# Pauses between the steps of the filling work, and a shorter second phase, in an FFT and GEGLU kernel

## The chip, the core and the metric

The kernel runs on one core of one Trainium2 chip. A core has a matrix engine (TensorE, PE in the profile, with its weight loads as PEld), three engines for elementwise work (VectorE or DVE, ScalarE or ACT, GpSimd or POOL), and SyncE (SP), from which this kernel issues nearly all its DMAs. Each engine works through a queue of its own, in the order in which the program wrote the instructions; the engines wait for each other by semaphores. The metric is the device time of one execution, in microseconds (us).

## What is computed

Two branches work on one input x of 8192 tokens by 448 channels, and their results are multiplied:

```python
x = A_x
xn = _layernorm(x, axis=-1)
s = _A_ref(xn, A_w1, A_b1, A_w2, A_b2)     # FFT over tokens, block MLP, inverse FFT
g = _silu(_B_ref(xn, B_w_gate, B_w_up, B_w_down))
return x + s * g

def _B_ref(x, w_gate, w_up, w_down):
    return (_gelu(x @ w_gate) * (x @ w_up)) @ w_down
```

`_A_ref` takes the real FFT over the 8192 tokens, runs a complex two-layer MLP in four blocks of 112 channels on every frequency (a ReLU between the layers, soft shrinkage by 0.01 behind them) and transforms back. `_B_ref` is a gated feed-forward network of width 1792. All products are formed from float16 pairs (a high and a low part), so that one float32 product is three matmuls or so.

## The kernel before

**Main work.** `ffn` runs the feed-forward network as 16 chunks of 512 tokens, in two passes over its width: p = 0 with 8 blocks of 128 columns, p = 1 with 6. Most chunks use Strassen-like products (`unit`), whose sums are formed on DVE, ACT and POOL, and a down projection (`down`, `down2`). Its tiles are `xta` and `xtb` (transposed tokens, fetched from the DRAM tensor `xts`), `wt` and `dw` (weights), `u`, `v`, `gl`, `wt` (intermediate sums), `h` (hidden values), `pt` and `th` (outputs). Its PSUM banks are six, named `bk`.

**Filling work.** Everything else is written into the gaps of the main work, with two PSUM banks named `bf`:

- Phase 1: `chunk1(c)` for c = 2 to 17 normalizes a chunk (`stats`, `norm`, tiles `st`, `x`, `xs`), forms its sums and stores them to `xts` (`factors`, tiles `sf`, `sx`), and does the first FFT stage (`stage1`: matmuls `bf<-xs,m`, results `ysb`, stored to `t1`). Chunks 16 and 17 are chunks 0 and 1 again, for `xts` alone. A chunk begins every DT = 40 us of the plan. Beside it `weights` prepares the second pass: `gu_block(b, 1)` for three blocks, `down_weights(1)`, and `prep_mlp` (MLP weights `w1t`, `w2t`); each of these calls begins when the one before it has ended.
- Phase 2 begins when both are done: `zero` for the first frequencies, then 64 calls of `group`, one every dt = (END2 - t0) / 64 (second FFT stage `bf<-sm,y`, MLP, shrinkage, third stage `bf<-vt,sm`).
- Phase 3: 32 calls of `tiles3` (last stage `bf<-u,mt`, product with the other branch in tile `g`, sum with x, store), one every dt = (END3 - t0 - 12) / 32. The last two leave `s4`, with which the main work's closing chain forms the last output.

**Who sets the order.** The whole program is written by one Python object, `Pace`, called the plan below. Every piece of work is a generator (a task). `Pace` keeps a modelled time for each engine, takes the task whose time comes first, lets it issue a few instructions, and puts it back: a bare `yield` means "go on when what I have just issued has ended in the model", `yield t` means "not before t", and `yield event` waits for another task. On the chip nothing of this exists: what remains is the order of the instructions in each engine's queue, and semaphores for true dependences. If the chip is later than the model at some place, an instruction may stand at the head of its queue with its operand not ready, and all behind it stand too. `SLACK` = 1.0 (line 26) is a margin of that kind for the `bf` banks (lines 415, 591 and 1571). `Either` (line 185) gives some elementwise operations to DVE or POOL, whichever would end first in the model. SP's DMAs go through the same plan.

**Lines that the change touches.** `Pace.__init__`, `spawn` and `run` (lines 54 to 101); `stage1` (585); END1, END2, END3 (1734); the loop of `phase3` that spawns `tiles3` (1802); `weights` (1914); `first` (1936), which spawns `chunk1`. Since every instruction is issued by the helper `Engine`, the profile gives line 180 (L180) for all of them; groups are told apart by tile names.

Of the kernel before, what the change touches and what calls it, by code (L numbers as in the profile page):

```python
# [21 lines left out]
NG = 16  # L22
CH = 4

PL = 2
SLACK = 1.0
BLK = ((0, 1), (1, 1)) + tuple((f, 2) for f in range(2, 14, 2))
NBK = len(BLK)

# [19 lines left out]
class Pace:  # L49
# [2 lines left out]


    def __init__(self):
        self.now, self.last, self.n, self.heap = 0.0, 0.0, 0, []
        self.free, self.seen, self.dma = {}, {}, 0.0


# [1 line left out]
        self.n += 1  # L60
        heapq.heappush(self.heap, (t, self.n, task))

    def spawn(self, gen, at=None):
        done = Event()

        def whole():
            yield from gen
            self.set(done)

        self.push(whole(), self.now if at is None else at)  # L70
        return done

    def then(self, fn, at=None):
# [12 lines left out]
    def run(self):  # L86
        while self.heap:
            t, _, task = heapq.heappop(self.heap)
            self.now = max(self.now, t)
            self.last = self.now  # L90
            try:
                y = next(task)
            except StopIteration:
                continue
            if isinstance(y, Event):
                if y.done:
                    self.push(task, self.now)
                else:
                    y.waiting.append(task)
            else:  # L100
                self.push(task, self.last if y is None else max(self.now, y))


    @staticmethod
# [279 lines left out]
def afno_geglu_kernel(ctx, tc, x, gu, wd, mlp, b1, b2, c_m, c_mt, c_small, out):  # L384
    nc = tc.nc
    pace = Pace()
# [27 lines left out]
    BX = BY = BD = Banks(pace, [psp.tile([128, 512], F32, name=f"bk{n}", bufs=1) for n in range(6)])  # L414
    BF = bank("bf", 2, SLACK)

    def part(bank_, *shape):

        n = int(np.prod(shape[1:]))
        v = bank_[0:shape[0], 0:n]  # L420
        return v.rearrange("p (a b) -> p a b", a=shape[1]) if len(shape) == 3 else v
# [25 lines left out]
    def block(f):  # L447
        return [f0 <= f < f0 + n for f0, n in BLK].index(True)

# [135 lines left out]
    def stage1(c, q, xs):  # L585
        if c >= PL:
            yield ev("lo", c, q)
        yield ev("m", c)
        m4 = EV["m4", c]
        ysb = yield from YS.get()  # L590
        yield pace.now + SLACK
        for a in range(2):
            b = yield from BF.get()
            py = part(b, 128, D)
            hi, lo = xs[:, a, 0], xs[:, a, 1]
            T.matmul(py, m4[:, 2 * q + a, 0, :], hi, start=True, stop=False)
            T.matmul(py, m4[:, 2 * q + a, 0, :], lo, start=False, stop=False)
            T.matmul(py, m4[:, 2 * q + a, 1, :], hi, start=False, stop=True)
            yield
            ph = py.rearrange("p (h d) -> p h d", h=2)  # L600
            S.activation(ysb[:, a, :, 0], ph, AF.Copy, scale=2.0 ** -16)
            yield
            V.scalar_tensor_tensor(ysb[:, a, :, 1], ph, 2.0 ** -16, ysb[:, a, :, 0], op0=ALU.mult, op1=ALU.subtract)
            BF.put(b)
        yield
        n2 = CH * c + 2 * q
        for ri in range(2):
            Q.dma_start(t1[:, ri, n2:n2 + 2, :], ysb[64 * ri:64 * ri + 64].rearrange("p a h s d -> p a (h s d)"))
        YS.put(ysb)

    def chunk1(c):

        yield ev("xl", c)
        yield from stats(c, G)
        yield
        tasks = []
        for q in range(2):
            xs = yield from XS.get()
            for a in (2 * q, 2 * q + 1):
                norm(c, a)  # L620
                yield
            xn = EV["x4", c][:, 2 * q:2 * q + 2, :]
            f = pace.spawn(factors(c, q, xs))
            S.copy(xs[:, :, 0, :], xn)
            yield
            B.tensor_sub(xs[:, :, 1, :], xn, xs[:, :, 0, :])
            pace.then(lambda c=c, q=q: done("lo", c, q))
            mine = [f]
            if c < NG:
                mine.append(pace.spawn(stage1(c, q, xs)))  # L630

            def back(mine=mine, xs=xs):
                for e in mine:
                    yield e
                XS.put(xs)

            tasks.append(pace.spawn(back()))
        yield tasks[0]
        yield tasks[1]
        done("xts", c % NG)  # L640
        X4.put(EV["x4", c])
        ST.put(EV["st", c])
        if c < NG:
            M4.put(EV["m4", c])
# [9 lines left out]
    T1, DT = 84.0, 40.0  # L654
# [11 lines left out]
    def gu_block(b, to):  # L666

        f0, n = BLK[b]
        for i in range(n):
# [867 lines left out]
    def layer1(n, w, z, h):  # L1537
# [32 lines left out]
        e = pace.spawn(other(), at)  # L1570
        yield pace.now + SLACK
        product(p0, 2, 1, False, True)
# [158 lines left out]

            pace.spawn(store())

    END1, END2, END3 = T1 + NG * DT + 12.0, 1480.0, 1780.0

    def phase2():
        yield ev("phase1")
# [36 lines left out]
    def tiles3(c):  # L1774
        yield ev("l3", c)
        t = EV["l3t", c]
        u2, mt = t[0:2]
        o2 = t[3] if c < 2 * NG - 2 else None
        for a in range(2):
            b = yield from BF.get()  # L1780
            p = part(b, 128, D)
            three(p, mt[:, a], u2[:, a, 0:D], u2[:, a, D:2 * D])
            yield
            if o2 is None:
                S.activation(state["last"][0][:, 2 * (c % 2) + a, :], p, AF.Copy, scale=cF)
                BF.put(b)
                yield
                done("s4", 2 * (c % 2) + a)
                continue
            V.scalar_tensor_tensor(o2[:, a, :], p, cF, o2[:, a, :], op0=ALU.mult, op1=ALU.mult)  # L1790
            BF.put(b)
            yield
            B.tensor_add(o2[:, a, :], o2[:, a, :], t[2][:, a, :])
            yield
        P3["u2"].put(u2)
        P3["mt"].put(mt)
        if o2 is not None:
            P3["x2"].put(t[2])
            Q.dma_start(ov[:, 2 * c:2 * c + 2, :], o2)
            P3["g2"].put(o2)  # L1800

    def phase3():
        r2.close()
        p3 = ctx.enter_context(tc.tile_pool(name="p3", bufs=1, side="right"))
        state["last"] = [p3.tile([128, CH, D], F32, name=n) for n in ("s4", "x4l")]
        for name, shape, dt, bufs in (("u2", [128, 2, 2 * D], F16, 3), ("mt", [128, 2, 3, 128], F16, 3),
                                      ("x2", [128, 2, D], F32, 3), ("g2", [128, 2, D], F32, 3)):
            P3[name] = ring(p3, shape, dt, name, bufs)
        n3 = 2 * NG
        order = list(range(n3))  # L1810
        t0 = pace.now
        dt = (END3 - t0 - 12.0) / n3
        pace.spawn(load3(order[0]))
        pace.spawn(load3(order[1]))
        Q.dma_start(state["last"][1], xv[:, CH * (NG - 1):, :])
        for k, c in enumerate(order):
            yield t0 + 10.0 + k * dt
            if k + 2 < n3:
                pace.spawn(load3(order[k + 2]))
            pace.spawn(tiles3(c))  # L1820


    p2 = None
# [90 lines left out]
    def weights():  # L1914

        near = range(PF[0][1])
        pace.spawn(gu_loads(near, 0))
        for b in range(PB[0][1]):
            pace.spawn(gu_block(b, 0))
        combs = pace.spawn(gu_combs(near))  # L1920
        yield ev("w", 1)
        yield pace.spawn(down_weights(0))
        yield combs
        yield 150.0
        for b in range(*PB[1]):
            yield pace.now + 10.0
            pace.spawn(gu_loads(range(BLK[b][0], sum(BLK[b])), 0))
            yield pace.spawn(gu_block(b, 1))
        yield pace.now + 10.0
        yield pace.spawn(down_weights(1))  # L1930
        far_rest()
        yield pace.last + 6.0
        yield pace.spawn(prep_mlp())
        done("weights")

    def first():
        G.memset(mhalf, -0.5)
        pace.spawn(begin())
        pace.spawn(weights())
        yield 0.0  # L1940
        S.activation(fb[:, 4:5], mhalf[:, 0:1], AF.Gelu_apprx_tanh)
        pace.spawn(load_m(0))
        pace.spawn(loads1())
        pace.spawn(ffn())
        tasks = []
        yield 28.0
        done("phase", 1)
        pace.spawn(begin1())
        for c in range(PL, NG + PL):
            done("phase", c - 1)  # L1950
            yield T1 + (c - PL) * DT
            if c > PL + 1:
                yield tasks[-2]
            tasks.append(pace.spawn(chunk1(c)))
        for e in tasks:
            yield e
        yield ev("weights")
        done("phase1")
        yield from phase2()
        yield from phase3()  # L1960
# [21 lines left out]
```

## Time and profile before

| what | us |
|---|---|
| median of three runs | 1845.62 |
| the three runs | 1842.31, 1845.62, 1846.54 |
| profiled execution, its own time | 1843.94 |
| profiled execution, span from first to last instruction | 1842.2 |
| mean granted TensorE clock of the profiled execution | 0.996 |

The profile page lists busy times for each engine; the trace behind it can be asked for stretches of time (busy times of each engine, granted clock, DMA), for waits (who stood for whom), for groups of equal instructions, and for single instructions in order of time. Times within the trace count from the span's start. An arrow `out<-in` names the tiles written and read. In lists of single instructions the first two numbers are start and duration, and brackets hold the idle time ahead of one and what ended it; `SPq`, in the place of an engine, is SyncE's sequencer issuing a DMA. In rows of groups, the numbers behind the bar are busy us in total, mean ns of one, and idle us of the engine just ahead of the group's instructions, with what ended it. Rows of one tile give shortest, median and longest duration in ns, then the first and last start in us.

### The profile page before, as it was taken

The numbers are of one execution on the slowest core, as the hardware profiler recorded it, in microseconds if no ns is written. First come the engines' busy times: TensorE is split into PE (matmuls) and PEld (weight loads), VectorE is DVE, ScalarE is ACT, GpSimd is POOL, SyncE is SP. The second block draws the span as 40 slices with busy tenths as digits, with TensorE's granted clock in tenths as the row PEclk, the third lists the DMA queues.
The fourth block names the chain that finished last, engine by engine and source line by source line (L and its number), as shares of the span: only waits on it lengthen the run. The fifth ranks groups of instructions, "written<-read, shape, count | busy, mean of one in ns | idle before, by whom it ended". The sixth has DMA issues, their size and how long they took to land. (4 is left out here: it accounts for less than half of the span.)

```text
span 1842.2 us, 39141 instructions
## 1 busy us (share of the span) xinstructions
PE 1774.8 (96%) x15649; PEld 1423.5 (77%) x15649; DVE 1423.4 (77%) x2418; ACT 1096.9 (60%) x2105; POOL 582.9 (32%) x629
## 2 busy tenths in 40 slices
PE   6999999999999999999999999999999999999997
PEld 3447567666777777887877899989989898878886
DVE  7867788776866666656767788888888897888888
ACT  4746566655655555566766777677777774434443
POOL 3334444324523313100101233334432342333332
PEclk9999999999999999999999999999999999999999
DMA  7463665586564552132235544543344435999984
GB/s 263 140 168 113 195 193 177 164 233 186 147 165 115 150 155 82 44 92 74 64 114 166 147 104 117 117 104 88 98 103 117 112 97 156 327 297 319 289 311 148
DMA packets 345655, 287.79 MB, mean 156 GB/s; under 512 B 231840, under 2 KB 312736, under 8 KB 345472
## 3 DMA queue, kind: packets, MB, share of 16 engines
q1 hardware_dynamic: 345328, 285.26, 53.9%
q8 instruction: 122, 2.00, 0.4%
q14 instruction: 61, 0.50, 0.1%
q10 hardware_dynamic: 144, 0.03, 0.0%
HBM read 129.47 MB, written 106.61 MB: 128 GB/s over the span
## 5 line engine op out<-in xcount | busy, mean ns | idle before, releaser
L180 PEld LDWEIGHTS <-wt 128*128 128x128 f16 x9350 | 908.7, 98 | 191.6 <-issue 26.6
L180 PE MATMUL bk<-xta,wt 128*128 128x256 f16 (+1 forms) x5190 | 635.2, 276 | 9.2 <-DVE wt L180 4.6
L180 PE MATMUL bk<-xtb,wt 128*128 128x256 f16 x3120 | 382.2, 273 | 7.7 <-ACT v L180 7.7
L180 PE MATMUL bk<-dw,h 128*128 128x448 f16 (+1 forms) x2208 | 375.1, 321 | 9.0 <-DVE h L180 4.1
L180 PEld LDWEIGHTS <-h 128*128 128x128 f16 x2688 | 257.8, 98 | 140.8 <-DVE h L180 5.7
L180 ACT COPY v<-bk 128x512 f32<-128x512 f32 x208 | 121.7, 585 | 100.6 <-PE bk L180 99.3
L180 ACT COPY u<-bk 128x512 f32<-128x512 f32 x208 | 121.2, 585 | 70.9 <-PE bk L180 65.2
L180 POOL TENSOR_TENSOR wt<-wt 128x256 f32<-128x256 f32 x92 | 81.2, 883 | 185.9 <-DVE wt L180 174.4
L180 DVE TENSOR_TENSOR u<-bk,u 128x512 f32<-128x512 f32 x104 | 71.3, 686 | 86.4 <-PE bk L180 85.9
L180 POOL TENSOR_TENSOR zs<-t,zs 112x256 f16<-112x256 f32 (+2 forms) x41 | 35.5, 865 | 303.4 <-ACT zs L180 297.7
L180 ACT ACTIVATE u<-u,fc 128x512 f32<-128x512 f32 (+1 forms) x118 | 77.7, 669 | 62.0 <-DVE u L180 61.6
L180 PE MATMUL bk<-dw,wt 128*128 128x224 f16 (+1 forms) x864 | 103.1, 269 | 8.1 <-DVE pt L180 8.0
L180 POOL TENSOR_TENSOR v<-v,u 128x512 f32<-128x512 f32 x40 | 61.2, 1531 | 156.5 <-ACT v L180 152.5
L180 DVE SCALAR_TENSOR_TENSOR pt<-bk,fb,pt 128x448 f32<-128x448 f32 x112 | 74.7, 677 | 32.9 <-PE bk L180 32.0
L180 ACT CAST h<-wt 128x512 f16<-128x512 f32 (+1 forms) x128 | 68.6, 538 | 48.7 <-DVE wt L180 36.3
L180 ACT ACTIVATE th<-bk,fb 128x448 f32<-128x448 f32 x64 | 40.5, 633 | 85.4 <-PE bk L180 59.8
L180 PE MATMUL bf<-w2t,wn 112*128 112x112 f16 x1512 | 84.9, 213 | 0.0
L180 PEld LDWEIGHTS <-wn 112*128 112x128 f16 x1512 | 80.6, 98 | 2.4
L180 DVE TENSOR_TENSOR v<-bk,v 128x512 f32<-128x512 f32 x104 | 71.0, 683 | 12.9 <-PE bk L180 11.4
L180 POOL TENSOR_TENSOR h<-wt,h 128x512 f16<-128x512 f32 (+1 forms) x50 | 62.8, 1260 | 39.7 <-ACT h L180 37.8
L180 PEld LDWEIGHTS <-w1t 112*112 112x112 f16 x612 | 68.1, 130 | 7.5 <-issue 2.9
L180 DVE TENSOR_SCALAR x<-x,st 128x448 f32<-128x448 f32 x72 | 56.0, 790 | 22.3 <-POOL st L180 22.1
(197 smaller groups left out, 2934.4 us busy)
## 6 DMA issues: line engine op xcount, KB each, us to landing
wst<-in_gu SPq DMA_DIRECT2D x22, 704.0 KB, 5.4
xts<-sx SPq DMA_DIRECT2D x32, 480.0 KB, 2.9
x<-in_x SPq DMA_DIRECT2D x17, 896.0 KB, 5.9
t<-ysb SPq DMA_DIRECT2D x64, 224.0 KB, 3.4
prt<-th SPq DMA_DIRECT2D x64, 224.0 KB, 2.6
pt<-prt SPq DMA_DIRECT2D x64, 224.0 KB, 4.4
u<-t SPq DMA_DIRECT2D x32, 448.0 KB, 5.6
y<-t SPq DMA_DIRECT2D x30, 448.0 KB, 3.5
```

The lines of the kernel that those rows point to most:

```text
L180: return self.pace.issue(self.name, kind, out, ins, lambda: fn(out, *args, **kw))
```

## The change

Each task gets a number `lag`, handed on to the tasks that it spawns unless another is given. A bare `yield` then means "go on `lag` us after what I have just issued has ended in the model". Tasks of the main work, the first two chunks, the weights of the first pass and phase 2 keep lag 0. `chunk1`, `gu_block(b, 1)`, `down_weights(1)` and `prep_mlp` get LAG = 1.0, with all that they spawn (`factors`, `stage1` and others); `tiles3` gets 0.5. In `stage1` the margin ahead of the bank gets the lag too, and behind each bank stands one more pause of that length. END2 goes from 1480 to 1460, so that the calls of `group` follow each other faster and phase 3 begins earlier, while END3 stays at 1780. No instruction is added or taken away.

```diff
--- before.py
+++ after.py
@@ -24,6 +24,7 @@
 
 PL = 2
 SLACK = 1.0
+LAG = 1.0
 BLK = ((0, 1), (1, 1)) + tuple((f, 2) for f in range(2, 14, 2))
 NBK = len(BLK)
 
@@ -52,7 +53,7 @@
 
 
     def __init__(self):
-        self.now, self.last, self.n, self.heap = 0.0, 0.0, 0, []
+        self.now, self.last, self.n, self.heap, self.lag = 0.0, 0.0, 0, [], 0.0
         self.free, self.seen, self.dma = {}, {}, 0.0
 
 
@@ -60,14 +61,14 @@
         self.n += 1
         heapq.heappush(self.heap, (t, self.n, task))
 
-    def spawn(self, gen, at=None):
+    def spawn(self, gen, at=None, lag=None):
         done = Event()
 
         def whole():
             yield from gen
             self.set(done)
 
-        self.push(whole(), self.now if at is None else at)
+        self.push((whole(), self.lag if lag is None else lag), self.now if at is None else at)
         return done
 
     def then(self, fn, at=None):
@@ -88,8 +89,9 @@
             t, _, task = heapq.heappop(self.heap)
             self.now = max(self.now, t)
             self.last = self.now
+            self.lag = task[1]
             try:
-                y = next(task)
+                y = next(task[0])
             except StopIteration:
                 continue
             if isinstance(y, Event):
@@ -98,7 +100,7 @@
                 else:
                     y.waiting.append(task)
             else:
-                self.push(task, self.last if y is None else max(self.now, y))
+                self.push(task, self.last + self.lag if y is None else max(self.now, y))
 
 
     @staticmethod
@@ -588,9 +590,11 @@
         yield ev("m", c)
         m4 = EV["m4", c]
         ysb = yield from YS.get()
-        yield pace.now + SLACK
+        yield pace.now + SLACK + pace.lag
         for a in range(2):
             b = yield from BF.get()
+            if pace.lag:
+                yield pace.now + pace.lag
             py = part(b, 128, D)
             hi, lo = xs[:, a, 0], xs[:, a, 1]
             T.matmul(py, m4[:, 2 * q + a, 0, :], hi, start=True, stop=False)
@@ -1731,7 +1735,7 @@
 
             pace.spawn(store())
 
-    END1, END2, END3 = T1 + NG * DT + 12.0, 1480.0, 1780.0
+    END1, END2, END3 = T1 + NG * DT + 12.0, 1460.0, 1780.0
 
     def phase2():
         yield ev("phase1")
@@ -1817,7 +1821,7 @@
             yield t0 + 10.0 + k * dt
             if k + 2 < n3:
                 pace.spawn(load3(order[k + 2]))
-            pace.spawn(tiles3(c))
+            pace.spawn(tiles3(c), lag=0.5)
 
 
     p2 = None
@@ -1925,12 +1929,12 @@
         for b in range(*PB[1]):
             yield pace.now + 10.0
             pace.spawn(gu_loads(range(BLK[b][0], sum(BLK[b])), 0))
-            yield pace.spawn(gu_block(b, 1))
+            yield pace.spawn(gu_block(b, 1), lag=LAG)
         yield pace.now + 10.0
-        yield pace.spawn(down_weights(1))
+        yield pace.spawn(down_weights(1), lag=LAG)
         far_rest()
         yield pace.last + 6.0
-        yield pace.spawn(prep_mlp())
+        yield pace.spawn(prep_mlp(), lag=LAG)
         done("weights")
 
     def first():
@@ -1951,7 +1955,7 @@
             yield T1 + (c - PL) * DT
             if c > PL + 1:
                 yield tasks[-2]
-            tasks.append(pace.spawn(chunk1(c)))
+            tasks.append(pace.spawn(chunk1(c), lag=LAG))
         for e in tasks:
             yield e
         yield ev("weights")
```

## The prediction

> **What bounds the kernel now.** The first view is the page's table of busy times, for the engine that is nearest to full.
>
> ```profile
> PE 1774.8 (96%) x15649; PEld 1423.5 (77%) x15649; DVE 1423.4 (77%) x2418; ACT 1096.9 (60%) x2105; POOL 582.9 (32%) x629
> ```
>
> TensorE (PE) is busy for 1774.8 of 1842.2 us, and the change takes no matmul away, so only the 67.4 us in which PE is idle, and stretches in which it runs slowly, can be won. The second view cuts the span at the borders of the three phases of the filling work. Its columns are the stretch, its length, the busy time of PE, its weight loads, DVE, ACT and POOL, then the granted clock and the DMAs.
>
> ```profile
> 150.00:490.00 340.00, 322.95 (x2421) 237.78 (x2420) 264.14 (x456) 198.93 (x360) 145.93 (x182) 0.98 0.60 175
> 490.00:742.00 252.00, 249.60 (x1891) 184.67 (x1891) 169.40 (x283) 134.24 (x241) 72.35 (x92) 1.00 0.51 135
> 742.00:1150.00 408.00, 408.00 (x4051) 343.70 (x4049) 293.24 (x517) 278.00 (x566) 68.20 (x64) 1.00 0.38 103
> 1150.00:1537.00 387.00, 381.57 (x4121) 350.61 (x4119) 332.16 (x555) 279.68 (x573) 149.76 (x138) 1.00 0.41 99
> 1537.00:1823.00 286.00, 272.58 (x2421) 234.65 (x2420) 237.38 (x352) 121.36 (x215) 95.60 (x84) 1.00 0.92 294
> 1823.00:1843.00 20.00, 8.12 (x78) 7.38 (x77) 12.83 (x22) 3.62 (x7) 0.00 (x0) 0.88 0.14 46
> ```
>
> Length less PE's time is PE's idle time: 17.1 us in 150 to 490 (5.0%), 2.4 us in 490 to 742 (1.0%), none in 742 to 1150, 5.4 us in 1150 to 1537 (1.4%), 13.4 us in 1537 to 1823 (4.7%), and about 11 us of closing chain. DVE is busy for 78%, 67%, 72%, 86% and 83% of the first five. So a full DVE alone doesn't stop PE: the fullest stretch costs 1.4%, a less full one 5.0%. The third view says what ended PE's idle time between 150 and 742.
>
> ```profile
> PE bf L180 <- DVE ysb L180: 4.0, 4, 1.9
> PE bk L180 <- ACT u L180: 2.7, 2, 1.7
> PE bk L180 <- POOL h L180: 2.6, 1, 2.6
> PE bk L180 <- ACT v L180: 2.1, 1, 2.1
> PE bf L180 <- DVE fx L180: 1.9, 2, 1.7
> PE bk L180 <- DVE h L180: 1.8, 2, 1.3
> PE bk L180 <- DVE wt L180: 1.5, 1, 1.5
> PE bf L180 <- DVE dmx L180: 1.3, 1, 1.3
> PE bf L180 <- DVE mxr L180: 1.2, 1, 1.2
> PE bf L180 <- DVE xs L180: 0.4, 1, 0.4
> ```
>
> The columns are who waited for whom, the sum in us, how often, and the longest. The `bf` rows are matmuls of the filling work itself, at which PE's queue stood: 4.0 + 1.9 + 1.3 + 1.2 + 0.4 = 8.8 us. The `bk` rows are the main work's matmuls, late because ACT, DVE or POOL came to their operand late: 2.7 + 2.6 + 2.1 + 1.8 + 1.5 = 10.7 us. One place in order of time, PE first and DVE second, shows how both arise.
>
> ```profile
> 184.81 0.61 PE L180 MATMUL bk<-xta,wt 128*128 128x256 f16 x4 [1.48 <-DVE wt L180]
> 187.31 1.30 PE L180 MATMUL bf<-xs,m 128*128 128x448 f16 x3 [1.89 <-DVE ysb L180]
> ```
>
> ```profile
> 184.67 2.04 DVE L180 TENSOR_TENSOR xs<-x,xs 128x896 f16<-128x896 f32 x1
> 186.64 0.61 DVE L180 SCALAR_TENSOR_TENSOR ysb<-bf,ysb 128x448 f16<-128x448 f32 x1
> ```
>
> DVE is back to back here. The `ysb` instruction, the last reader of a `bf` bank, starts only at 186.64, and the filling matmul that wants the bank was written into PE's queue on the plan's belief that it would be free. PE, with main work behind, stands for 1.89 us.
>
> **The change part by part.** No instruction is added or removed, and no wait: a pause in the plan only puts a step at a later place in its engines' queues, DMAs and SP's queue included. Nothing is queued behind a pause.
>
> **1. Pauses in the first phase, matmuls of the filling work.** A step written 1 us later finds its operand ready if the chip runs up to 1 us behind the plan; `stage1` gains 2 us before its first matmul, the plain pause at line 591 and the new one behind the bank. The four `ysb` waits, longest 1.9, should go nearly all. `fx`, `dmx` and `mxr` get 1 us against longest waits of 1.7, 1.3 and 1.2. That alone leaves about 1.3 of 8.8 us; new waits of the kind will arise at other places. Bounds: 0 and -8.8; I take two thirds, **-6.0**.
>
> **2. The same pauses, main matmuls.** With filling steps spread, ACT, DVE and POOL meet fewer filling instructions in a row ahead of a main one. It is a matter of order, and DVE's total stays. Bounds: 0 and -10.7; I take less than half, **-4.0**, as only some of these bursts are the filling work's own.
>
> **3. The clock.** Two stretches of the first phase have a low granted clock (the last figure but two).
>
> ```profile
> 184.00:196.00 12.00, 9.31 (x55) 6.50 (x56) 9.34 (x13) 6.55 (x14) 6.07 (x6) 0.72 0.33 93
> 443.00:451.00 8.00, 6.50 (x26) 3.04 (x27) 4.72 (x8) 3.12 (x6) 2.29 (x4) 0.79 0.56 164
> ```
>
> ```profile
> 444.50 0.36 PE L180 MATMUL bk<-dw,h 128*128 128x448 f16 x1 [2.60 <-POOL h L180]
> ```
>
> They cost 0.28 x 12 + 0.21 x 8 = 5.0 us of PE time, and each follows idle PE: 1.48 and 1.89 us in the first, 2.60 us for POOL's `h` in the second. Fewer stalls should leave fewer of these. Bounds 0 and -5.0; I take half, **-2.5**.
>
> The Trainium skill, "TensorE: Matmul & The Clock Gate", section "What's actually happening", has the clock halve after at least one idle window of about 3.4 us. The trace doesn't agree as it stands: no idle piece before these two stretches is longer than 2.6 us. By that rule such short stalls cost no clock, this term would be 0, and the sum below 2.5 us higher.
>
> **4. Later ends in the first phase.** The pauses add up along a task. The last `chunk1` (c = 17) has about 18 pauses in a row: six through `stats`, two at `norm`, four in the first `factors` while it holds the one SF buffer, six in the second and its stores. For the weights: about 31 in each of three `gu_block` calls, 40 in `down_weights(1)`, 25 in `prep_mlp`, or 158 us in all.
>
> ```profile
> 505.16 0.68 DVE L180 SCALAR_TENSOR_TENSOR w2t<-raw,ms,w2t 112x448 f16<-112x448 f32 x1
> ```
>
> ```profile
> L180 PE MATMUL bf<-sm,y x768: 216/219/222, 742.4 to 1509.6; 128*112 128x128 f16 x189, 128*112 128x130 f16 x3
> ```
>
> ```profile
> 790.30 0.83 PE L180 MATMUL bf<-sm,y 128*112 128x128 f16 x12
> ```
>
> The weights now end at 505 and would end near 663, still before the second phase's first matmul at 742.4; that one moves by the chunk's 18 us to about 760. So weight work moves into 490 to 742, where PE is idle for 1.0% only. At worst that stretch takes on the 5.0% of the one before it: 252 x 4.0% = +10.1 us; at best its 2.4 us go. I take **+2.0**, nearest to its own row, since DVE has room there (67%).
>
> Nobody on PE waits for the later chunks:
>
> ```profile
> 195.22 2.32 SPq L180 DMA_DIRECT2D xts<-xs  x4
> ...
> 254.76 4.00 SPq L180 DMA_TRANSPOSE xta<-xts  x1
> ```
>
> The transposed data of chunk 4 are stored by 198 and fetched at 254.76, when the buffer comes free. The cover is some 57 us against about 18 us of pauses; without it, each us of excess would stand on PE.
>
> **5. The denser second phase.** Its groups begin at 790.30 and the last at 1509.6: 719.3 / 63 = 11.42 us a group. A start 18 us later and END2 20 us earlier make that (719.3 - 38) / 63 = 10.81 us, 5.6% more filling work per us. Between 1150 and 1537 half of DVE's work is the filling work's: ten groups from the first row below to the last sum to 182 us, and the ten of the main work to 184.
>
> ```profile
> L180 DVE SCALAR_TENSOR_TENSOR vt<-vt,o 128x448 f16<-128x448 f16 (+1 forms) x35 | 25.8, 737 | 4.6 <-ACT vt L180 4.5
> ...
> L180 DVE TENSOR_TENSOR zs<-t,zs 112x256 f16<-112x256 f32 x9 | 4.2, 466 | 1.4 <-ACT zs L180 1.4
> ```
>
> So DVE goes from 86% to about 88%. Bounds: -1 (the first half starts later) and the third phase's 4.7% over 387 us, 18.2 - 5.4 = +12.8. I take **+2.5**, half as much again as now, because the stretch's own row is the nearest and DVE stays below full.
>
> **6. The third phase, pause 0.5 us and an earlier start.**
>
> ```profile
> L180 PE MATMUL bf<-u,mt x192: 349/352/362, 1558.4 to 1822.5; 128*128 128x448 f16 x192
> ```
>
> ```profile
> PE bk L180 <- DVE pt L180: 6.8, 17, 1.5
> PE bk L180 <- ACT v L180: 5.6, 4, 2.5
> ```
>
> ```profile
> L180 DVE SCALAR_TENSOR_TENSOR g<-bf,ms,g 128x448 f32<-128x448 f32 x60 | 40.5, 677 | 12.4 <-PE bf L180 11.2 <-DMA g<-gsp 1.2
> L180 DVE TENSOR_TENSOR g<-g,x 128x448 f32<-128x448 f32 x42 | 33.4, 796 | 0.6
> ```
>
> END3 stays, so its tiles have 284 us in place of 264.1, 7% fewer per us, and the DMAs (0.92 busy in that stretch) as much relief. `g` is 73.9 us of DVE's work, 26% of 286 us, so DVE falls by about 2 points. PE waits for main operands (`pt`, `v`) here, not for filling matmuls, so the pause itself does little. Bounds: down to the 1.4% of the stretch before it, 4.0 - 13.4 = -9.4, and +3 if pauses push the last tile into the closing chain (some six of 0.5 us). I take **-3.0**.
>
> The choice between DVE and POOL for one instruction (Either) is made afresh with each new time; that can go either way and is left at nothing, inside the bounds of 2 and 5.
>
> **Sum:** -6.0 - 4.0 - 2.5 + 2.0 + 2.5 - 3.0 = -11.0 us. The profiled execution took 1843.94 us (1842.2 span and 1.7 around it), so 1832.9; the median of the three runs, 1845.62, lies 1.7 above it, so **1834.6**, told as 1835.
>
> **The rivals.** *Stalls only move.* DVE's total and PE's order of main work stay, so a burst avoided here meets another there. For it: POOL's and ACT's waits are scattered, no place repeats. Against it: 8.8 us stand at filling matmuls whose steps get later by more than most of those waits. Time: that of before, 1844 to 1846. That the pauses leave the queues' order nearly as it is, since the plan had room there already, ends at the same time.
>
> *The second phase becomes the place that stalls.* Mechanism: at 88% DVE falls behind the plan between 1150 and 1537, main products wait for `u`, `v`, `pt`, and the stretch takes the third phase's rate, +12.8. With half of points 1 to 3 (-6.2) and nothing from the third phase: 1843.9 + 6.6 + 1.7 = 1852, slower. It decides from the point where the stretch gains about 10 us of idle time. For it: 1.4% at 86% beside 4.7% at 83% shows how fast that can turn. Against it: 72% to 86% of DVE has cost only 5.4 us.
>
> *Nearly all of the first phase comes back.* Points 1 to 3 at 85% of their bounds, -20.8, with the other points as above, +1.5: 1826. For it: most `bk` waits too have filling work ahead of them in the queue. Against: point 2 has no rule that protects a main matmul.
>
> **How the numbers follow.** The forecast has 0.50, the full recovery 0.15, stalls that move 0.18, queues left nearly as they are 0.05, the stalling second phase 0.12. A measurement of this kernel tells 0.2%, 3.7 us, from no change. Faster takes the first two and a little of the moving stalls, less the forecast's weak edge: 0.66; same 0.20; slower 0.14. The range 1822 to 1850 takes in the full recovery and what lies between the forecast and the stalling second phase.
>
> **What would show it.** Right: the waits for `ysb`, `fx`, `dmx`, `mxr` under 3 us together; idle PE in 150 to 490 under 9 us; the weights' last `w2t` near 660 and the first `bf<-sm,y` near 760; the first `bf<-u,mt` near 1540 and its stretch under 11 us idle. Wrong: new waits of main matmuls between 490 and 742, over 10 us of idle PE between 1150 and 1537, or a closing chain that is longer than 11 us.

## The result, and the profile after

| | us |
|---|---|
| changed kernel, median of four runs (1817.71 to 1823.30) | 1819.38 |
| kernel before, median of four runs beside it (1842.31 to 1846.54) | 1844.35 |
| ratio, 95% interval | 0.9867, 0.9854 to 0.9881 |
| profiled execution of the changed kernel, its own time and span | 1818.44, 1816.3 |

The change makes the kernel 1.3% faster, 25 us. The forecast was 1835, and the lower end of its range, 1822, lies 2.6 us above the measured time. The page's table of busy times for the changed kernel:

```profile
PE 1768.8 (97%) x15649; PEld 1422.6 (78%) x15649; DVE 1401.5 (77%) x2410; ACT 1098.1 (60%) x2105; POOL 588.0 (32%) x637
```

PE's count is the same; its idle time is 1816.3 - 1768.8 = 47.5 us in place of 67.4. The stretches, cut at this kernel's own phase borders (columns as in the prediction):

```profile
150.00:490.00 340.00, 333.18 (x2547) 248.13 (x2546) 268.37 (x474) 204.57 (x369) 131.13 (x166) 1.00 0.60 174
490.00:735.00 245.00, 244.70 (x1869) 183.04 (x1868) 166.03 (x298) 138.98 (x252) 84.91 (x101) 1.00 0.56 158
735.00:1150.00 415.00, 413.39 (x4115) 348.81 (x4114) 303.34 (x541) 288.37 (x584) 66.53 (x63) 1.00 0.38 101
1150.00:1515.00 365.00, 362.60 (x3936) 333.71 (x3934) 310.68 (x513) 263.18 (x541) 152.25 (x143) 1.00 0.42 103
1515.00:1801.00 286.00, 278.07 (x2475) 239.64 (x2474) 235.12 (x345) 124.94 (x221) 106.20 (x101) 1.00 0.92 292
```

Idle PE is 6.8, 0.3, 1.6, 2.4 and 7.9 us, where it was 17.1, 2.4, 0, 5.4 and 13.4. The low clock of the first stretch (0.98 before) is gone. What PE waited for between 150 and 742:

```profile
PE bk L182 <- ACT u L182: 4.8, 2, 3.4
PE bk L182 <- DVE wt L182: 0.9, 1, 0.9
PE bk L182 <- ACT wt L182: 0.7, 1, 0.7
PE bk L182 <- DVE h L182: 0.3, 1, 0.3
PE bk L182 <- ACT v L182: 0.3, 1, 0.3
```

Not one `bf` row is left: in this stretch PE stands at no matmul of the filling work any more. Rows of tiles and two instructions give the dates of the phases:

```profile
649.24 0.68 DVE L182 SCALAR_TENSOR_TENSOR w2t<-raw,ms,w2t 112x448 f16<-112x448 f32 x1
```

```profile
L182 PE MATMUL bf<-sm,y x768: 217/219/222, 734.8 to 1487.5; 128*112 128x128 f16 x189, 128*112 128x130 f16 x3
```

```profile
787.05 0.83 PE L182 MATMUL bf<-sm,y 128*112 128x128 f16 x12
```

```profile
L182 PE MATMUL bf<-u,mt x192: 352/352/363, 1535.9 to 1800.6; 128*128 128x448 f16 x192
```

The weights end at 649 (505 before). The second phase begins at 734.8, earlier than the 742.4 of before; its groups follow each other every (1487.5 - 787.05) / 63 = 11.12 us (11.42 before). The third phase's matmuls spread over 264.7 us, just as before (264.1).

Idle time leaves out half-clock stretches, so the experiments are compared by **lost time**: for each matmul the time to the next one's start, less the usual step of its shape in the trace of before (109 ns for 256 columns, 189 ns for 448), summed over a phase. "First" runs from 150 us to the first `bf<-sm,y`, "second" from there to the last `bf<-vt,sm`, "third" from there to the last matmul. "Half clock" is the part of the whole loss that is due to a halved clock. How the usual step is taken shifts a sum by up to 1 us.

| kernel | first | second | third | half clock | median us | ratio to before, 95% |
|---|---|---|---|---|---|---|
| before | 29.4 | 10.1 | 20.8 | 5.1 | 1844.35 | |
| the change | 10.9 | 8.2 | 14.0 | 0 | 1819.38 | 0.9867 (0.9854 to 0.9881) |
| e1 pauses of phase 1 alone | 15.1 | 11.5 | 18.0 | 3.4 | 1827.07 | 0.9889 (0.9870 to 0.9907) |
| e2 END2 alone | 28.4 | 9.9 | 23.4 | 5.1 | 1847.80 | 1.0007 (0.9998 to 1.0017) |
| e3 pause in tiles3 alone | 32.0 | 10.1 | 19.8 | 10.2 | 1842.52 | 0.9987 (0.9974 to 1.0000) |
| e4 pauses of chunk1 alone | 16.0 | 10.1 | 30.2 | 8.5 | 1839.27 | 0.9966 (0.9951 to 0.9981) |
| e5 pauses of the weights alone | 18.0 | 17.5 | 22.9 | 8.5 | 1843.35 | 0.9988 (0.9979 to 0.9998) |
| e6 stage1's two pauses alone | 26.6 | 12.2 | 28.4 | 8.5 | 1853.94 | 1.0048 (1.0032 to 1.0064) |
| e7 chunk1's steps without those two | 15.5 | 11.4 | 19.2 | 3.4 | 1829.99 | 0.9924 (0.9908 to 0.9940) |
| e8 two long pauses per chunk | 26.8 | 14.1 | 19.7 | 8.5 | 1843.59 | 0.9993 (0.9978 to 1.0008) |
| e19 weights apart, no pause | 28.2 | 8.3 | 22.1 | 6.8 | 1847.43 | 1.0010 (0.9999 to 1.0021) |
| e12 LAG 0.5 | 28.2 | 15.5 | 17.1 | 10.2 | 1847.93 | 1.0009 (1.0000 to 1.0018) |
| e18 LAG 1.1 | 20.2 | 12.1 | 13.3 | 6.8 | 1834.24 | 0.9935 (0.9921 to 0.9950) |
| e11 LAG 2.0 | 15.3 | 25.1 | 70.7 | 42.7 | 1902.89 | 1.0309 (1.0291 to 1.0326) |
| e9 the change, no pause in tiles3 | 13.2 | 8.3 | 23.0 | 3.4 | 1831.52 | 0.9920 (0.9905 to 0.9935) |
| e20 the change, 0.4 in tiles3 | 14.2 | 8.1 | 11.4 | 3.4 | 1817.74 | 0.9847 (0.9831 to 0.9864) |
| e21 the change, 0.6 in tiles3 | 13.4 | 8.2 | 16.6 | 1.7 | 1822.54 | 0.9873 (0.9858 to 0.9888) |
| e10 the change, END2 1480 | 13.5 | 11.4 | 18.5 | 1.7 | 1834.14 | 0.9933 (0.9919 to 0.9948) |
| e16 the change, END2 1470 | 13.1 | 14.5 | 16.2 | 1.7 | 1827.84 | 0.9904 (0.9887 to 0.9920) |
| e15 the change, END2 1450 | 14.1 | 23.8 | 19.9 | 6.8 | 1843.11 | 0.9987 (0.9976 to 0.9998) |

Each lost time is of one profiled execution, which can lie some us from its kernel's median: e3's took 1848.18 us, 5.7 above, e15's 4.2 above. Each ratio is to runs of the kernel before on the same chip. Eight of these kernels (the change, e1, e9, e10, e15, e16, e20, e21) have PE's order in the first phase in common, and lose 10.9 to 15.1 us there: that is how far one order scatters, and differences below 4 us within a phase say nothing. The lost time of the change and of before differs by 18.5, 1.9 and 6.8 us in the three phases, 27.2 in all, of which some 1.6 go back in the first 84 us.

### The profile page after: what moved, and what is told of

It reads as the page before. It is cut to its first block, busy times and chain, and to the rows that moved or that the text cites. A ratio compares the mean times of both kernels' runs of the same rounds, so it can differ in the third digit from the quotient of the medians.

```text
span 1816.3 us, 39111 instructions
## 1 busy us (share of the span) xinstructions
PE 1768.8 (97%) x15649; PEld 1422.6 (78%) x15649; DVE 1401.5 (77%) x2410; ACT 1098.1 (60%) x2105; POOL 588.0 (32%) x637
## 5 line engine op out<-in xcount | busy, mean ns | idle before, releaser
L182 PEld LDWEIGHTS <-wt 128*128 128x128 f16 x9350 | 907.0, 98 | 181.8 <-issue 18.5
L182 POOL TENSOR_TENSOR zs<-t,zs 112x256 f16<-112x256 f32 (+2 forms) x34 | 30.0, 884 | 262.0 <-ACT zs L182 258.7
L182 DVE TENSOR_TENSOR v<-bk,v 128x512 f32<-128x512 f32 x104 | 71.2, 684 | 19.7 <-PE bk L182 19.1
L182 POOL TENSOR_TENSOR v<-v,u 128x512 f32<-128x512 f32 x32 | 47.5, 1485 | 97.1 <-ACT v L182 96.9
L182 ACT ACTIVATE th<-pt 128x448 f32<-128x448 f32 x64 | 36.8, 576 | 58.8 <-DVE pt L182 48.9
L182 DVE SCALAR_TENSOR_TENSOR gl<-v,fc,gl 128x512 f32<-128x512 f32 (+1 forms) x70 | 47.1, 690 | 32.4 <-ACT gl L182 31.0
```

Of the source, the lines that this page charges most:

```text
L182: return self.pace.issue(self.name, kind, out, ins, lambda: fn(out, *args, **kw))
```

## The experiments

All edits below are to the changed kernel. "END2 back" stands for `1460.0` becoming `1480.0`.

### The change in three parts

```diff
e1: END2 back;  -pace.spawn(tiles3(c), lag=0.5)  +pace.spawn(tiles3(c))
e2: -LAG = 1.0  +LAG = 0.0;  tiles3 as in e1
e3: -LAG = 1.0  +LAG = 0.0;  END2 back
```

> Pauses of the first phase alone (chunk1 and weights), END2 back at 1480, tiles3 without a pause. The stretches of the two profiles give the first phase some 18 us of the 26 us gain and the third some 6 to 7. If the gain is the first phase's own and the parts add up, this kernel takes 1824 to 1829 us. Rival: the third phase gains because the first does (the main work arrives elsewhere): then nearly all is here, 1817 to 1822 us.

> END2 at 1460 alone, no pause anywhere. If thinner filling work in the third phase is what helps there, 1838 to 1842 us, with less idle PE behind the second phase's end and no more than 3 us more within it. Rival, that the pause of 0.5 us does it: 1843 to 1848 us, as the denser second phase then only costs.

> The pause of 0.5 us in tiles3 alone, END2 at 1480. If thinner filling work is what helps in the third phase: 1843 to 1846 us, no difference. Rival, that the pause does it: 1838 to 1841 us.

e1 took 1827.07, within the theory's 1824 to 1829: most of the gain is the first phase's. e2 took 1847.80, in its rival's range and against the theory that a second phase which ends earlier thins the third; its third phase does spread more (1549.1 to 1821.9, 272.8 us) and still loses 23.4 us. e3 took 1842.52, between both ranges. Alone, these two parts are worth +2 and -3 us or so; together, on top of the first, they are worth -8. So the parts don't add up, and the third phase was taken up again below.

### Chunks, weights, and stage1's margin

```diff
e4: END2 back, tiles3 as in e1; gu_block(b, 1), down_weights(1), prep_mlp without lag=LAG
e5: END2 back, tiles3 as in e1; chunk1 without lag=LAG
e6: END2 back, tiles3 as in e1; -LAG = 1.0  +LAG = 0.0
-        yield pace.now + SLACK + pace.lag
+        yield pace.now + SLACK + (c > 1)
-            if pace.lag:
-                yield pace.now + pace.lag
+            if c > 1:
+                yield pace.now + 1.0
e7: as e4, and stage1 as in the kernel before
```

> Pauses in chunk1 alone, not in the weights. If the chunks' steps carry the gain of the first phase: 1826 to 1832 us. Rival, that the weights' work, stretched from 505 to about 650 us, carries it: 1838 to 1843 us.

> Pauses in the second pass's weights alone, none in chunk1. In the profile of the chunks alone PE's lost time between 150 us and the second phase is already as low as with both, so the weights' pauses should bring little there: 1840 to 1846 us. Rival, that the thinner weights' work is what the chunks alone lacked (6.7 us less against 18.9 with both): 1832 to 1837 us.

> Only the two pauses of 1 us ahead of stage1's matmuls, for c > 1; no step of any task is paused otherwise, END2 at 1480. If the waits of PE at filling matmuls are the larger part (point 1 of the prediction): the 4.0 us for ysb and their share of half clock go, 1838 to 1841 us. Rival, that the main matmuls' waits carry the gain: 1843 to 1846 us.

> Pauses in chunk1's steps as in e4, but without the two pauses ahead of stage1's matmuls. If readiness of the operands of elementwise steps on ACT, DVE and POOL carries the first phase's gain: idle PE between 150 us and the second phase at most 4 us above e4, 1837 to 1844 us. Rival, that stage1's pauses carry it: idle PE back at 17 us or more in that stretch and 1843 to 1847 us.

e4 took 1839.27, short of the theory's range and in the rival's, but not for the rival's reason, since its first phase is as good as that of both together (16.0 and 15.1 us). Its third phase loses 30.2. e5 took 1843.35, as expected, and for another reason than expected: its first phase falls to 18.0 too, and the second and third lose 9.5 us more than before. Either set of pauses brings most of the first phase's gain, and what one of them earns can be given back later.

e6 took 1853.94, out of both ranges, and slower than before. The waits for `ysb` shrink, and the wait for another filling matmul grows in their place (PE's waits of e6 between 150 and 725):

```profile
PE bf L182 <- DVE fx L182: 7.9, 2, 4.1
...
PE bf L182 <- DVE ysb L182: 1.5, 2, 1.0
```

e7, without these two pauses, took 1829.99, less than its expectation and less than e4, with the same first phase. No wait for `ysb` is left in it, though 5.4 us at other filling matmuls are. So the margin ahead of stage1's matmuls is not what helps most; the pauses at the steps of the elementwise work are.

### Is it the stretching?

```diff
e8: END2 back, tiles3 as in e1, LAG = 0.0; in chunk1
         yield from stats(c, G)
-        yield
+        yield pace.last + 8.0
         tasks = []
         for q in range(2):
+            if q:
+                yield pace.now + 10.0
e19: as e1, with no lag in chunk1 or the weights; in weights
-            yield pace.now + 10.0
+            yield pace.now + (10.0 if b == PB[1][0] else 41.0)
...
-        yield pace.now + 10.0
+        yield pace.now + 41.0
         yield pace.spawn(down_weights(1))
         far_rest()
-        yield pace.last + 6.0
+        yield pace.last + 46.0
```

> No pause at the steps; instead each chunk1 waits once 8 us behind its statistics and once 10 us between its halves, so that a chunk is stretched by as much as 18 pauses do. If stretching, that is fewer filling steps in a row, is what helps: idle PE between 150 us and the second phase falls from 19 to 12 us or less, as in e4. Rival, that each step must find its operand ready: idle PE stays at 16 us or more there, with the waits for ysb and fx in place, 1842 to 1848 us.

> No pause anywhere; the second pass's weights are instead prepared in pieces 31 us further apart, so that they end as late as with pauses. If thinner weights' work is what the weights' pauses bring: lost time between 150 and 490 at 18 us or less, as with those pauses alone (14.8). Rival, that their steps' readiness brings it: 23 to 27 us there.

Both stretch the work as the pauses do, in a few large pieces. e8's time (1843.59) is the rival's; its idle PE, 15.1 us from 150 to 725, lies between the two limits, and its first phase loses 26.8. For the weights the comparison is plain. First e5 (pauses), then e19 (apart), in the stretches 150 to 490 and 490 to 725:

```profile
150.00:490.00 340.00, 330.96 (x2520) 245.74 (x2519) 260.14 (x435) 198.10 (x360) 142.04 (x178) 0.99 0.56 165
490.00:725.00 235.00, 233.05 (x1751) 171.19 (x1749) 170.09 (x297) 134.09 (x240) 76.43 (x101) 1.00 0.57 157
```

```profile
150.00:490.00 340.00, 327.81 (x2477) 242.69 (x2475) 253.58 (x428) 195.37 (x354) 140.34 (x171) 0.98 0.54 159
490.00:725.00 235.00, 229.07 (x1740) 170.36 (x1738) 174.88 (x317) 132.46 (x239) 64.75 (x92) 1.00 0.56 153
```

e19's weights end about as late (632 us, e5's 643), and PE is idle for 12.2 + 5.9 us, against 9.0 + 1.9 with pauses. Between 150 and 490 e19 loses about 21 us, between the two limits of its expectation, but in the whole phase 28.2, where before lost 29.4: thinning only moved the loss. So coarse stretching is not the cause; it takes pauses at the single steps. PE's waits at filling matmuls show the same: 8.8 us before, 9.4 in e6, 7.9 in e8, 6.4 in e19, and none with pauses at every step of both sets. Whether such a pause helps because the step's operand is ready or because a main instruction gets in between two filling ones was not told apart, as a pause does both.

### The length of the pause

```diff
e12: -LAG = 1.0  +LAG = 0.5
e18: -LAG = 1.0  +LAG = 1.1
e11: -LAG = 1.0  +LAG = 2.0
```

> The change with pauses of 0.5 us. If a step has to find its operand ready, waits at filling matmuls of 0.5 us and more partly return: lost time between 150 and 490 of 14 to 20 us, 1822 to 1832 us. Rival, that any change of order does it: no relation to the length, below 13 us or above 22 us.

> The change with pauses of 1.1 us, as small an edit as can be. If the change's 1819 us are what its parts earn, 1817 to 1823 us. If its third phase fell together well by the order drawn: the first phase's gain stays (lost time between 150 and 490 within 3 us of the change) while the rest moves by 5 us or more, 1824 to 1840 us.

> The change with pauses of 2 us instead of 1 in the first phase. If a step only has to find its operand ready, 1 us is enough already (the waits of PE at filling matmuls are gone at 1): the first phase's lost time stays at 9 to 13 us between 150 and 490, and longer tasks push the second phase later, into its jam: 1825 to 1850 us. Rival, that stretching pays by its length: lost time there down to 7 us or less and 1812 to 1819 us.

At 0.5, 1.0, 1.1 and 2.0 us the first phase loses 28.2, 10.9 to 15.1, 20.2 and 15.3 us, in no relation to the length. From 0.5 us on, no wait at a filling matmul is left in that stretch; what differs are the main work's waits, that for ACT's `u` above all: 16.1 us in e12, its longest 7.6. That stall, first ACT and then PE:

```profile
221.76 0.63 ACT L182 ACTIVATE th<-bk,fb 128x448 f32<-128x448 f32 x1 [4.97 <-DMA prt<-th]
```

```profile
223.91 1.44 PE L182 MATMUL bk<-xta,wt 128*128 128x256 f16 x6 [7.63 <-ACT u L182]
```

ACT stands at `th`, a main output, until the store of an earlier `th` to `prt` has landed and freed its buffer, and `u` waits behind it. Three of PE's waits in e12, 7.63, 6.00 and 1.46 us, stand behind such a stall of ACT; with the 8.5 us of half clock that follow them they make 23.6 of e12's 28.2 us. The changed kernel's own longest stall is of this kind (ACT, SP, PE):

```profile
387.02 1.18 ACT L182 ACTIVATE th<-bk,fb 128x448 f32<-128x448 f32 x2 [10.00 <-DMA prt<-th]
```

```profile
377.80 10.74 SPq L182 DMA_DIRECT2D prt<-th  x4
```

```profile
388.72 0.49 PE L182 MATMUL bk<-xta,wt 128*128 128x256 f16 x3 [3.45 <-ACT u L182]
```

The SP row holds four issues. The first store was issued 4.7 us after its `th` was written, since SP's queue was issuing other DMAs up to then, and the slowest of the four took 9.1 us to land, where the median of all stores to `prt` is 2.0. That a pause of the filling work can't cure such a stall is argued, not tried.

So e12 has what was expected of it between 150 and 490 (about 17 us lost), but loses 11 more behind that, and its time misses 1822 to 1832 by 16 us. e18 lies in its second range in time, but not for the reason given there: its first phase moved (about 5 us more than the change between 150 and 490, 9.3 in all), and the third kept its gain. A pause longer by a tenth thus costs half of the change's gain (0.65% faster than before in place of 1.33%), so part of that gain is luck: how well this one order happens to fall. e11 loses about 13 us between 150 and 490, as expected, but its time is 53 us past its range. It shows the limit of the pause. Its weights end at 809.84, so that the second phase begins late, and the third is pressed into 212 us in front of a fixed END3 (rows of its tiles, then its stretch 1652 to 1886 and PE's waits there):

```profile
L182 PE MATMUL bf<-u,mt x192: 352/353/581, 1673.6 to 1886.0; 128*128 128x448 f16 x192
```

```profile
1652.00:1886.00 234.00, 185.12 (x1421) 139.31 (x1418) 160.53 (x240) 65.03 (x117) 60.13 (x54) 0.84 0.94 314
```

```profile
PE bf L182 <- DMA mt<-c_mt: 25.3, 11, 4.3
PE bf L182 <- DVE g L182: 19.2, 8, 5.9
```

PE waits for loads of the filling work, the clock falls to 0.84, and the kernel is 57 us slower than before. The first phase itself gained about as much as with 1 us.

### What END2 and the third phase's pause do on top

```diff
e9:  tiles3 without lag        e20: lag=0.4        e21: lag=0.6
e10: END2 1480.0               e16: END2 1470.0    e15: END2 1450.0
```

> The change without the pause in tiles3. Theory: the third phase's 7 us come from the thinner filling work there (END2 earlier), on top of the first phase: 1819 to 1823 us. Rival: the pause of 0.5 us carries them: 1826 to 1832 us. Third: neither does by itself, the third phase's loss depends on how the two orders happen to fall together: anything from 1817 to 1834 us, not the sum of the parts.

> The change with a pause of 0.4 us in tiles3 in place of 0.5; the order of all work ahead of the third phase stays. If the pause earns the third phase's gain (12.9 us lost there against 21.9 without it): 1819 to 1823 us. If 0.5 drew a good order by chance: the loss there anywhere from 13 to 25 us, 1824 to 1832 us.

> The same with 0.6 us. If the pause earns the gain: 1816 to 1821 us. If 0.5 drew a good order by chance: 1824 to 1832 us, and not in line with 0.4 and 0.5.

PE's order up to the end of the second phase is the same in these three and in the change. Without the pause the third phase loses 23.0 us (21.9 from the first `bf<-u,mt` on, as the expectations count it); with 0.4, 0.5 and 0.6 us it loses 11.4, 14.0 and 16.6, and the medians are 1831.52, 1817.74, 1819.38 and 1822.54. So here the pause earns 9 to 14 us, and 0.4 does as well as 0.5. e9 is in its rival's range; e20 lies 1.3 us below the range of a pause that earns the gain and e21 1.5 above it, and neither in the range of chance. PE's waits behind 1515, first of e9, then of e20:

```profile
PE bk L182 <- DVE pt L182: 8.0, 16, 2.0
PE bk L182 <- DVE h L182: 4.5, 4, 1.9
PE bk L182 <- ACT h L182: 2.2, 3, 1.2
```

```profile
PE bk L182 <- DVE pt L182: 2.6, 13, 0.2
PE bk L182 <- DVE h L182: 2.4, 3, 1.0
PE bk L182 <- ACT v L182: 1.4, 2, 1.2
```

The main work waits about as often for DVE's `pt`, and far shorter: 0.2 us at the longest in place of 2.0.

> The change with END2 back at 1480. Theory (thinner third phase): 1825 to 1829 us, as with the first phase's pauses alone. Rival (the pause of 0.5 us): 1818 to 1822 us. Third (how the orders fall together): not the sum of the parts, up to 1834 us.

> The change with END2 at 1470. If thinner filling in the third phase pays steadily: between the change and the one with 1480, some 2 to 4 us above the change, 1821 to 1824 us. Rival, that END2 only draws another order: up or down by several us, not between its neighbours.

> The change with END2 at 1450 in place of 1460. If thinner filling in the third phase pays steadily: 1816 to 1819 us, the lost time of the third phase down by 1 to 3 us more. Rival, that END2 only draws another order: up or down by several us, with the third phase's lost time anywhere from 13 to 27 us.

By END2 the medians are 1834.14 (1480), 1827.84 (1470), 1819.38 (1460) and 1843.11 (1450). With the pause in tiles3, an earlier end pays down to 1460, though 1470 lies 4 us above what steady thinning was expected to give, and 1480 is the third case of its expectation, at the upper end. Without the pause, 1460 is slower than 1480 (e9 1831.52, e1 1827.07). Nor is the filling work thinner: the third phase's matmuls spread over 264.7 us at 1480 as at 1460. With 1480 the last tile of the third phase ends too late for the closing chain:

```profile
L182 PE MATMUL bf<-u,mt x192: 352/352/363, 1553.6 to 1818.3; 128*128 128x448 f16 x192
```

That is PE's last matmul in e10, and 11.4 us follow it, where before and the change have 8.4. At 1450, in its rival's case, the second phase stalls (rows of its groups, then its two halves):

```profile
L182 PE MATMUL bf<-sm,y x768: 217/219/222, 738.9 to 1528.4; 128*112 128x128 f16 x189, 128*112 128x130 f16 x3
```

```profile
739.00:1150.00 411.00, 406.45 (x4032) 341.43 (x4031) 293.66 (x520) 277.68 (x564) 70.23 (x66) 1.00 0.38 100
1150.00:1553.00 403.00, 390.68 (x4198) 358.26 (x4197) 338.92 (x568) 279.10 (x575) 139.91 (x134) 1.00 0.41 101
```

Asked to follow faster, the groups follow slower: the last one begins at 1528.4, 41 us later than with 1460, and PE is idle for 4.6 + 12.3 us, where the change has 1.6 + 2.4. DVE is no fuller (84% in the second half). Half of this idle time, 8.8 us in 11 waits, stands at filling matmuls that wait for DVE's `k`, a step of the MLP's first layer in `group`, where the change has 2.0 us in 4. That is the kind of wait that the pauses took out of the first phase, and the tasks of the second have no pause. Whether pauses there would help was not tried.

## Why the prediction was right or wrong, point by point

- **What bounds the kernel**: right. The whole gain is idle and slow PE time, and the lost time accounts for it.
- **Point 1**, waits at filling matmuls: right in kind, mis-sized. Two thirds of 8.8 us were taken (-6.0); all of it went, and no new wait of the kind arose in the phase. The reason given for the larger part, `stage1`'s two pauses, fell: e6 has them alone and only swaps `ysb` for `fx`, and e7 has no `ysb` wait without them.
- **Point 2**, main matmuls: right in size, -4.0 forecast, 10.7 to 7.0 us measured. Half of what is left is one wait for a DMA (`prt`, 3.45 us), which the prediction did not see. DVE's total did not stay, as the point says it would: it fell from 1423.4 to 1401.5 us, with 8 instructions fewer (Either gave them to POOL) and a mean of 582 ns in place of 589. That is not what sets the time: e16 has 1402.2 us and is 8 us slower than the change, and e11, with 1409.3, is slower than before.
- **Point 3**, the clock: mis-sized. Half of 5.0 us was taken; in the profiled execution all of it went. In the first phase of the other seven kernels with this order half clock costs 1.7 to 3.4 us, so half was not far off. The prediction's reading that each low stretch follows its idle pieces is refined below: in the first, the clock was halved at 186.0, before the 1.89 us piece had ended.
- **Point 4**, later ends: the dates of the weights were right (663 forecast, 649 measured), the cost was not: +2.0 forecast for 490 to 742, -2.1 measured (2.4 to 0.3 us idle). The second phase did not move to 760 but to 734.8. In PE's order it did move back, by 88 main matmuls (4818 stand ahead of it, 4730 before), some 10 us; but the whole main work arrives 18 us earlier. A shift in the plan was added to a date of the chip. The chunks' slack for `xts` held.
- **Point 5**, the denser second phase: wrong sign at this size, +2.5 forecast, 1.9 us less lost time, which is within the scatter. Groups follow every 11.12 us, not 10.81. The mechanism itself is real and close by: at END2 1450 it costs what the rival of the stalling second phase foresaw (16.9 us of idle PE there, 1843), and with LAG 0.5 the second phase loses 15.5 us.
- **Point 6**, the third phase: wrong reason. END2 was to thin it from 264.1 to 284 us; it stayed at 264.7. The pause, said to do little there, does the work: -9 to -14 us beside e9. It does so only with END2 at 1460: at 1480 the third phase loses 18.5 us with it (e10) and 18.0 without (e1). What the point says of the closing chain holds in e10.
- **The rivals**: "nearly all of the first phase comes back" was the case nearest to what came, at 1826 and 0.15; its -20.8 us for points 1 to 3 stand beside 18.5 us measured for the phase. It kept the forecast's small terms for the other two phases, and 1.9 + 6.8 us came from these.

In sum: the first phase was undersized by 8.0 us (10.5 forecast, 18.5 lost time saved), the second by 4.4, and the third by 3.8, for a wrong reason. The step that failed first is thus the share taken of points 1 to 3, two thirds, less than half and half of their bounds, where 18.5 us of lost time went. That alone would have given about 1826; the rest, down to 1819, is point 5, which had the wrong sign, and point 6, which was too small and gave the gain to the wrong part of the change. Why the third phase's pause pays at END2 1460 and costs at 1480 (e10 against e1, 1834.14 and 1827.07) is shown only in part: the two profiled executions differ by 2.7 us, which is the closing chain's 3 us; the other 4 us of the medians stand in no trace, and why the pause gains nothing in the phase itself at 1480 stays open.

## What to carry to other kernels

Where a plan in advance fixes the order of in-order queues, a step that is due exactly when its operand is due in the model stands at the head of the queue on the chip whenever the chip is late: a pause of 1 us at every background step bought 1% here, and large pauses at a few places bought nothing. The length is not safe to choose by reason alone: 0.5 us took out the same waits, but another stall ate the gain, and 1.1 us kept half of it. Such a pause has to be paid for from the slack of the phase, so follow the sum of the pauses to the phase's end; past it, with pauses of 2 us, the kernel was 57 us slower than before. Judge parts of a reordering together and by phase: alone, two of these parts were worth +2 and -3 us, and the first phase's gain was given back later in two variants.

## What the hardware did that was not expected

One and the same stall, 3.4 to 4.2 us of idle PE, stands near 389 in the eight kernels with the first phase's order in common. Their stretch 385 to 398, for the change, e9 and e1 in turn:

```profile
385.00:398.00 13.00, 9.55 (x83) 7.67 (x81) 12.18 (x23) 8.22 (x17) 2.78 (x3) 1.00 0.35 117
```

```profile
385.00:398.00 13.00, 9.03 (x65) 6.60 (x63) 8.04 (x14) 5.29 (x11) 1.32 (x2) 0.87 0.55 188
```

```profile
385.00:398.00 13.00, 9.02 (x55) 6.21 (x53) 9.14 (x16) 6.13 (x12) 1.32 (x2) 0.74 0.40 137
```

Granted clock 1.00, 0.87 and 0.74: no half clock, 3.4 us of it, and 6.8 us, or a cost of 0, 1.7 and 3.4 us for one and the same stall. The traces show what decides. All changes of the granted clock within one execution lie on a grid of 3.413 us: in the kernel before, the two drops at 186.04 and 445.46 are 76 steps apart. Take every step of that grid between 150 us and the last matmul in the twenty traces, and add up PE's idle time in each. Of the steps at full clock, 50 are followed by a step at half clock, and these hold 1.73 to 3.41 us of idle PE; the 9685 others hold at most 1.99 us. So it is the idle time summed within one step that counts, with the border between 1.7 and 2.0 us, and not the length of one stall. The change's stall, from 385.27 to 388.72, is cut by the grid at 386.9, which leaves 1.6 and 1.85 us in its two steps: no half clock. In the kernel before, the stall of 1.48 us and the first 0.6 us of the one of 1.89 fall into one step, 2.1 us together, and the clock halves at its end.

The Trainium skill, "TensorE: Matmul & The Clock Gate", section "What's actually happening", says that the window of about 3.4 us runs freely. The grid of 3.413 us agrees with that, and so does the different cost of one and the same stall from trace to trace. Its rule that the clock halves after at least one idle window does not, if such a window has to be idle throughout: 1.73 us of idle PE in a step was enough in e7, at 1577.
